# mLSTM scan and MLP on one core: two groups more with divided words, one copy in place of two halves, and a new written order

## The chip, the cores and the metric

The kernel runs on one core of a Trainium2 chip. The metric is device time in microseconds (us). Before the change the median of three runs is 465.06 us (464.52 to 466.18). The engines are TensorE (PE, with its weight loads apart as PEld), VectorE (DVE), ScalarE (ACT), GpSimd (POOL) and SyncE (SP), whose queue issues most DMA transfers.

## What is computed

The first half is a recurrent attention with gates, for 4 batches, 8 heads, 768 steps and a head size of 40:

```python
m_new = maximum(f[t] + m, i[t])
f_stab, i_stab = exp(f[t] + m - m_new), exp(i[t] - m_new)
C = f_stab * C + i_stab * outer(v[t], k[t])
n = f_stab * n + i_stab * k[t]
y[t] = sigmoid(o[t]) * (C @ q[t]) / maximum(abs(n . q[t]), 1)
```

The second half takes the 3072 rows of y, 320 wide, through two layers:

```python
h = x @ w_in            # 320 x 2048
g = h * erf(softplus(h))
out = g @ w_out         # 2048 x 320
```

w_in and w_out come as 64-bit floats, whose two 32-bit words the kernel turns into float32 itself.

## The kernel before

The scan is cut into 12 steps `k` of 64 time steps. In each step `attention` works on batch rows 0 and 1 and then on rows 2 and 3: scores, masks, products with the carried state, and the state's update. Its result is divided, gated, turned on PE and kept as `xh` and `xl`, a rounded part and the rest. `mlp(g)` takes a quarter `q` of the 2048 hidden columns for one step, so there are four groups to a step; for steps 0 and 1 they alternate (`k, q = g % 2, g // 2`). A group multiplies up (L764, "up"), copies to `hb` (ACT L775), takes softplus (ACT L784), erf (ACT L788) and the product (DVE L792), and multiplies down into a sum over four groups ("dn"), for two halves `b` of 128 rows each.

A down multiplication has two forms, and `PLAIN` chooses. Groups below it use float32 words whole, four matmuls a half (L828). The others divide their words first: `gh` is `n0` rounded (ACT L802, or DVE L804 from group 32 on) and `gl` is the rest (DVE L808). Then eight matmuls "hi" of a half take `gh` with both parts of w_out (L832, L833) and four "lo" take `gl` with w_out's rounded part (L830). w_out's blocks are divided by `split_out`, all 16 of them. The sums of a step lie in the PSUM tiles `pob0` and `pob1`, but that of step 1 lies in a buffer of the pool `pa`, of which there are two; the scores, products and turned results use the same two.

The order of the work is written out. `Plan` collects some 1,590 operations with the engine and the dependences of each; `ORDER` (L94 on) lists their numbers, and `plan.run` emits them in that order. Each engine works through its own instructions in that order, and waits where a needed one is not done. A negative number stands for filler matmuls (`stay`, L910). ACT's functions come from tables; where the next operation needs another one, a table load (L913) is emitted.

The startup: `gate_block` makes the gates' sums of two steps (DVE L311 to L317), which go through DRAM (`gd`, L378) to be spread as masks `dm` and factors `eT`. `weights_in` and `weights_tail` turn w_in's words (DVE L640, ACT L646, DVE L651) and split them into `wh` (ACT) and `wl` (DVE L665, L703). `vg` (DVE L495) is the gated v, L578 masks scores, `qe` (DVE L478) is q with its factors, L516 the state's matmuls, L405 makes `xl`'s part of a turned result. `kvo` (L439) is one transfer of k, v and the output gate.

At the end of a step each half of the sum is copied to SBUF on ACT (L859) and stored in two pieces on SP's queue (L865). For the second half of the last step there is another way: ACT copies 160 columns (L844) and issues a store on its own queue (L845), DVE copies the others (L849), and SP stores them (L853).

Of the kernel before, what the change touches and what calls it, by code (L numbers as in the profile page):

```python
# [17 lines left out]
L = 64  # L18
# [15 lines left out]
class Plan:  # L34
# [135 lines left out]
def tile_mlstm_moe(  # L170
# [561 lines left out]
    def mlp(g):  # L732
# [77 lines left out]
        for b in range(2):  # L810
# [24 lines left out]
            if q == 3:  # L835
                def rows(x, b):
                    return x.rearrange("(b s) e -> b s e", s=S)[2 * b:2 * b + 2, k * L:(k + 1) * L]

                if k == NC - 1 and b == 1:
                    half = DM // 2  # L840

# [133 lines left out]
```

## Time and profile before

| what | before |
|---|---|
| median of three runs | 465.06 us |
| lowest, highest | 464.52, 466.18 us |
| the profiled execution's own time | 466.24 us |
| its span, first to last instruction | 464.5 us |
| mean granted TensorE clock | 0.983 |
| busy in the span: PE, ACT, DVE, POOL | 450.7, 338.0, 334.0, 38.3 us |
| matmuls | 6000 |

How to read it: the busy time of an engine is the time in which it had an instruction at work; a PE that is busy may still run at the lower clock. The chain is followed back from the last instruction, at each step to what released it. The granted clock is a share of the full one, 2.4 GHz. Line numbers are those of the kernel before; in the new kernel they are one higher, and 20 lower behind the removed lines.

### The profile page before, as it was taken

Reading aid. Unit: us, or ns where it says so; the run is one execution under the profiler, and the core shown is the slowest. Engines: PE = TensorE matmul, PEld = TensorE weight load, DVE = VectorE, ACT = ScalarE, POOL = GpSimd, SP = SyncE. Lnnn points to the kernel's source line nnn. Section 1 sums busy time; section 2 is a strip of 40 time slices with the busy share of each in tenths; the row PEclk is TensorE's granted clock in tenths of the full one; section 3 lists DMA queues with packets and bytes.
Section 4 is the critical chain, followed back from the end, with each engine's and each line's share of the span. In section 5 each row is a group of like instructions: output and inputs, shape, how many; then the busy total and the mean of one; then the engine's idle time right before and its main releaser. Section 6 shows DMA issues by size and latency. Waiting matters only on the chain.

```text
span 464.5 us, 13909 instructions
## 1 busy us (share of the span) xinstructions
PE 450.7 (97%) x6000; PEld 405.0 (87%) x6000; DVE 334.0 (72%) x658; ACT 338.0 (73%) x530; POOL 38.3 (8%) x64
## 2 busy tenths in 40 slices
PE   6989998999999999999999999999999999999995
PEld 4669996788899998999999898899899889999994
DVE  5889788854878667887766867786678885567651
ACT  4568997966998875786877695987866776776550
POOL 4002010012120020003102000104001000000000
PEclk9879998999999999999999999999999999999999
DMA  7899595671841112147160464015522100000111
GB/s 212 326 276 344 167 251 193 178 256 28 250 129 49 48 39 78 22 135 191 30 181 0 107 214 126 3 48 155 135 71 65 31 1 17 14 2 8 22 30 28
DMA packets 46930, 51.80 MB, mean 112 GB/s; under 512 B 27028, under 2 KB 31764, under 8 KB 46868
## 3 DMA queue, kind: packets, MB, share of 16 engines
q1 hardware_dynamic: 46738, 50.83, 37.5%
q8 instruction: 47, 0.77, 0.7%
q14 instruction: 15, 0.12, 0.1%
q10 hardware_dynamic: 130, 0.08, 0.1%
HBM read 46.77 MB, written 4.13 MB: 110 GB/s over the span
## 4 chain that ended last, share of the span: by engine, by line
PE 94%; DVE 2%; DMA 2%; ACT 1%; issue 1%; DVEq 0%
PE h L764 40%; PE pob L832 11%; PE pob L830 11%; PE pob L833 10%; PE pa L536 3%; PE pa L828 3%; PE pa L516 3%; PE pa L507 2%; PE pa L521 2%; PE pob L828 2%; DMA kvo<-in_kvo_dram 1%; PE pa L388 1%; PE pa L444 1%; PE pob L282 1%; PE pa L529 1%
## 5 line engine op out<-in xcount | busy, mean ns | idle before, releaser
L764 PE MATMUL h<-xh,wh 128*128 128x256 f32 (+1 forms) x768 | 202.2, 347 | 0.1
L764 PEld LDWEIGHTS h<-xh,wh 128*128 128x128 f32 x768 | 127.6, 193 | 13.5 <-DVE hb L780 0.5
L775 ACT ACTIVATE hb<-h 128x256 f32<-128x256 f32 (+1 forms) x160 | 66.5, 421 | 69.9 <-PE h L764 69.6
L764 PE MATMUL h<-xh,wl 128*128 128x256 f32 x384 | 109.2, 284 | 0.0
L832 PE MATMUL pob<-woh,gh 128*128 128x320 f32 x328 | 98.8, 313 | 0.0
L833 PE MATMUL pob<-wo,gh 128*128 128x320 f32 x328 | 97.5, 309 | 0.0
L780 DVE TENSOR_TENSOR hb<-h,hb 128x256 f32<-128x256 f32 x128 | 52.3, 420 | 48.3 <-ACT hb L775 47.2
L913 ACT ACT_TABLE_LOAD x62 | 79.5, 1283 | 1.8 <-PEq L963 0.8
L764 PEld LDWEIGHTS h<-xh,wl 128*128 128x128 f32 x384 | 73.8, 192 | 2.3 <-DVE wl L665 0.2
L792 DVE TENSOR_TENSOR n<-n,hb 128x1024 f32<-128x1024 f32 x48 | 58.3, 1219 | 14.6 <-ACT n L788 14.4
L833 PEld LDWEIGHTS pob<-wo,gh 128*128 128x128 f32 x328 | 61.7, 188 | 1.5
L832 PEld LDWEIGHTS pob<-woh,gh 128*128 128x128 f32 x328 | 61.8, 188 | 0.7
L830 PE MATMUL pob<-woh,gl 128*128 128x320 f32 x328 | 60.7, 311 | 0.0
L485 POOL TENSOR_SCALAR_AFFINE_SELECT dm<-dm 128x512 f32<-128x512 f32 (+1 forms) x40 | 32.6, 821 | 311.0 <-ACT dm L465 279.1
L830 PEld LDWEIGHTS pob<-woh,gl 128*128 128x128 f32 x328 | 52.3, 188 | 1.6
L808 DVE TENSOR_TENSOR gl<-n,gh 128x1024 fp32r<-128x1024 f32 x42 | 51.6, 1230 | 1.1 <-ACT gh L802 0.7
L784 ACT ACTIVATE n<-hb 128x1024 f32<-128x1024 f32 x48 | 50.0, 1058 | 1.9 <-DVE hb L780 1.5
L788 ACT ACTIVATE n<-n 128x1024 f32<-128x1024 f32 x48 | 49.9, 1055 | 0.3
L802 ACT ACTIVATE gh<-n 128x1024 fp32r<-128x1024 f32 x26 | 27.1, 1057 | 0.7 <-DVE n L792 0.7
L405 DVE TENSOR_TENSOR xh<-pa,xh 128x384 fp32r<-128x384 f32 x24 | 13.3, 554 | 19.1 <-ACT xh L401 19.1
L536 PEld LDWEIGHTS pa<-kvo,dm 64*32 64x32 f32 x1408 | 15.6, 109 | 4.3 <-issue 3.7
L578 DVE TENSOR_TENSOR dm<-pa,dm 128x512 f32<-128x512 f32 x22 | 15.0, 683 | 5.8 <-PE pa L507 5.2
(103 smaller groups left out, 486.3 us busy)
## 6 DMA issues: line engine op xcount, KB each, us to landing
qk<-in_qk_dram SPq DMA_DIRECT2D x24, 512.0 KB, 3.7
kvo<-in_kvo_dram SPq DMA_DIRECT2D x24, 484.0 KB, 5.2
eT<-gd SPq DMA_DIRECT2D x44, 128.0 KB, 3.7
raw<-in_w_out_dram SPq DMA_DIRECT2D x16, 320.0 KB, 7.4
dm<-gd SPq DMA_DIRECT2D x40, 128.0 KB, 3.2
raw<-in_w_in_dram SPq DMA_DIRECT2D x8, 512.0 KB, 8.1
out_dram<-o SPq DMA_DIRECT2D x47, 80.0 KB, 2.1
raw<-in_w_in_dram SPq DMA_DIRECT2D x4, 256.0 KB, 7.4
```

The source lines that it names most:

```text
L485: nc.gpsimd.affine_select(out=x, in_=x, pattern=[[0, H], [1, L]], compare_op=ALU.is_ge, fill=0.0, base=base, channel_multiplier=-1)
L764: nc.tensor.matmul(h[:, n * T:n * T + n_], w, m, start=(s == 0), stop=(s == len(ops) - 1))
L775: nc.scalar.activation(part(), G(f'h{i}')[:, T:2 * T] if wide else G(f'h{i}'), AF.Copy)
L780: nc.vector.tensor_tensor(part(), G(f'h{i}')[:, 0:T], part(), op=ALU.add)
L784: nc.scalar.activation(new('n0', [128, 1024], ('n0', g)), G('hb'), AF.Softplus)
L788: nc.scalar.activation(G('n0'), G('n0'), AF.Erf)
L792: nc.vector.tensor_tensor(G('n0'), G('n0'), G('hb'), op=ALU.mult)
L808: nc.vector.tensor_tensor(new('gl', [128, 1024], ('gl', g), F32R), G('n0'), G('gh').bitcast(F32), op=ALU.subtract)
L830: nc.tensor.matmul(acc(b), G('gl')[:, ts], woh[:, j], start=False, stop=(j == NFF - 1))
L832: nc.tensor.matmul(acc(b), G('gh')[:, ts], woh[:, j], start=(j == 0), stop=False)
L833: nc.tensor.matmul(acc(b), G('gh')[:, ts], t['wol', j], start=False, stop=False)
L913: plan.run(ORDER, lambda k: nc.scalar.preload_act_table_set(KIND[k]), stay)
```

## The change

`PLAIN` goes from 6 to 4: groups 4 (step 0) and 5 (step 1), third quarter, now divide their words. With `PLAIN` the places move where `split_out` is written: blocks 8 to 15 ahead of group 4, and 0 to 7 behind group 7. The other way of the last half's copy is taken out. `ORDER` is written anew throughout; it has four filler matmuls in place of three, and it makes 62 table loads in place of 61.

```diff
 ORDER = [
-    2, 10, 4, 41, 0, 5, 9, 12, 1, 13, 6, 3, 7, 14, 15, 8, 16, 11, 17, 33, 34, 32, 36, 31, 25, 343, 344, 20, 27, 28, 18, 35, 19,
...
+    0, 5, 2, 1, 3, 41, 7, 9, 11, 12, 13, 14, 15, 4, 20, 25, 31, 6, 16, 10, 8, 17, 351, 352, 33, 34, 26, 27, 28, 30, 24, 38, 37,
...
 ]
-PLAIN, JOIN, GH_ACT, FLAT = 6, 3, 32, 1
+PLAIN, JOIN, GH_ACT, FLAT = 4, 3, 32, 1
...
-                def rows(x, b):
-                    return x.rearrange("(b s) e -> b s e", s=S)[2 * b:2 * b + 2, k * L:(k + 1) * L]
-
-                if k == NC - 1 and b == 1:
-                    half = DM // 2
-
-                    @op('ACT', 0.2, r=[(po(b), b)], w=[(('o', k, b), 0)], tile_=('o', ('o', k, b)))
-                    def _(b=b):
-                        nc.scalar.activation(new('o', [128, DM], ('o', k, b))[:, 0:half], acc(b)[:, 0:half], AF.Copy)
-                        nc.scalar.dma_start(rows(out, b)[:, :, 0:half], t['o', k, b][:, 0:half])
-
-                    @op('DVE', 0.2, r=[(po(b), b)], w=[(('o', k, b), 1)], tile_=())
-                    def _(b=b):
-                        nc.vector.tensor_copy(t['o', k, b][:, half:DM], acc(b)[:, half:DM])
-
-                    @dma(320, mm=8, r=[(('o', k, b), 1)])
-                    def _(b=b):
-                        nc.sync.dma_start(rows(out, b)[:, :, half:DM], t['o', k, b][:, half:DM])
-
-                    continue
-
```

The order moves at two places that matter below. The first is DVE in the startup. Before, this is what stands there up to the low part of w_in's columns 0 to 511, rows 0 to 127 (`raw_408`); `raw_303` holds rows 128 to 255 of these columns, `raw_251` the tail rows 256 to 319, `raw_487` and `raw_495` the next columns:

```order
L578 TENSOR_TENSOR dm_321<-pa_333,dm_321 128x2x4x64
L623 SCALAR_TENSOR_TENSOR kvo_157<-kvo_157 128x320
L495 TENSOR_TENSOR vg_387<-kvo_385,dm_325 128x328
L578 TENSOR_TENSOR dm_325<-pa_353,dm_325 128x2x4x64
L478 TENSOR_TENSOR qe_393<-qk_327,eT_390 104x512
L405 TENSOR_TENSOR xh_280<-pa_395,xh_280 128x3x128
L665 TENSOR_TENSOR wl_74<-raw_303,wh_73 128x512
L640 TENSOR_SCALAR raw_408<-raw_408 128x512
L703 TENSOR_TENSOR wh_73<-raw_251,wh_73 64x512
L651 SCALAR_TENSOR_TENSOR raw_408<-raw_408 128x512
L405 TENSOR_TENSOR xh_280<-pa_412,xh_280 128x3x128
```

Now, with `raw_277` and `raw_322` for the two parts of the same columns, `raw_261` for the tail and `raw_378` and `raw_381` for the next columns:

```order
L496 TENSOR_TENSOR vg_332<-kvo_328,dm_330 128x328
L406 TENSOR_TENSOR xh_297<-pa_334,xh_297 128x3x128
L666 TENSOR_TENSOR wl_74<-raw_277,wh_73 128x512
L406 TENSOR_TENSOR xh_297<-pa_345,xh_297 128x3x128
L641 TENSOR_SCALAR raw_322<-raw_322 128x512
L479 TENSOR_TENSOR qe_356<-qk_343,eT_353 104x512
L579 TENSOR_TENSOR dm_330<-pa_358,dm_330 128x2x4x64
L704 TENSOR_TENSOR wh_73<-raw_261,wh_73 64x512
L641 TENSOR_SCALAR raw_378<-raw_378 128x512
L652 SCALAR_TENSOR_TENSOR raw_322<-raw_322 128x512
L652 SCALAR_TENSOR_TENSOR raw_378<-raw_378 128x512
L641 TENSOR_SCALAR raw_381<-raw_381 128x512
```

The two `xh` operations stand ahead of the first `wl`, one gated v and one masked score in place of two stand ahead of them, and the second `wl`, from `raw_322`, follows right behind these rows.

The second place is SP's queue around the load of step 2's kvo for batch rows 0 and 1. Before, it is `kvo_1038`; `gd4` are the stores of the gates of steps 4 and 5, `raw` the loads of w_out, `gt` a load of gates:

```order
L378 DMA gd4_851<-x_775 8x4x64
L292 DMA gt_889<-in_gates_dram 128x2x128
L473 DMA eT_891<-gd2_402 64x8x64 x2
L435 DMA qk_894<-in_qk_dram 128x2x512
L473 DMA eT_949<-gd2_402 64x8x64 x2
L711 DMA raw_1021<-in_w_out_dram 128x640
L711 DMA raw_1024<-in_w_out_dram 128x640
L456 DMA dm_1034<-gd2_402 64x512 x2
L378 DMA gd4_851<-x_775 8x4x64
L439 DMA kvo_1038<-in_kvo_dram 128x968
```

Now it is `kvo_1139`:

```order
L712 DMA raw_964<-in_w_out_dram 128x640
L436 DMA qk_1089<-in_qk_dram 128x2x512
L379 DMA gd4_1108<-x_750 8x4x64
L474 DMA eT_1110<-gd2_723 64x8x64 x2
L293 DMA gt_1132<-in_gates_dram 128x2x128
L379 DMA gd4_1108<-x_750 8x4x64
L712 DMA raw_1137<-in_w_out_dram 128x640
L440 DMA kvo_1139<-in_kvo_dram 128x968
```

Two stores of gates stand ahead of the load in either order; one of the two mask and factor loads went elsewhere, and a w_out load stands directly ahead.

## Rows read from the trace of the kernel before

**Rows 1.** The page: busy time by engine, and shares of the last chain.
```profile
PE 450.7 (97%) x6000; PEld 405.0 (87%) x6000; DVE 334.0 (72%) x658; ACT 338.0 (73%) x530; POOL 38.3 (8%) x64
...
PE 94%; DVE 2%; DMA 2%; ACT 1%; issue 1%; DVEq 0%
```

**Rows 2.** Stretches: length, busy of PE, PEld, DVE, ACT, POOL, clock, DMA share, GB/s.
```profile
50.00:60.00 10.00, 10.00 (x110) 9.80 (x110) 7.88 (x18) 9.92 (x20) 0.00 (x0) 1.00 0.46 111
...
70.00:80.00 10.00, 7.87 (x154) 6.65 (x154) 8.32 (x19) 7.49 (x14) 0.00 (x0) 0.84 0.57 194
250.00:260.00 10.00, 10.00 (x146) 8.88 (x145) 7.46 (x13) 7.01 (x15) 2.91 (x4) 1.00 0.14 34
...
29.03:35.86 6.83, 6.83 (x145) 6.43 (x142) 6.56 (x13) 4.90 (x11) 0.00 (x0) 0.50 0.96 220
76.80:80.20 3.40, 3.40 (x17) 3.40 (x18) 2.99 (x7) 3.38 (x9) 0.00 (x0) 0.50 0.71 231
```

**Rows 3.** The chain of waits: start, length, what; an up, and down pieces.
```profile
82.46 1.91 PE h L764 x16
84.37 2.15 PE pa L828 x8
...
457.10 0.15 PE pob L832
...
458.28 0.60 PE pob L830 x4
```

**Rows 4.** The page's groups: operation, count, busy, mean ns, idle before it.
```profile
L913 ACT ACT_TABLE_LOAD x62 | 79.5, 1283 | 1.8 <-PEq L963 0.8
...
L792 DVE TENSOR_TENSOR n<-n,hb 128x1024 f32<-128x1024 f32 x48 | 58.3, 1219 | 14.6 <-ACT n L788 14.4
...
L808 DVE TENSOR_TENSOR gl<-n,gh 128x1024 fp32r<-128x1024 f32 x42 | 51.6, 1230 | 1.1 <-ACT gh L802 0.7
L784 ACT ACTIVATE n<-hb 128x1024 f32<-128x1024 f32 x48 | 50.0, 1058 | 1.9 <-DVE hb L780 1.5
L788 ACT ACTIVATE n<-n 128x1024 f32<-128x1024 f32 x48 | 49.9, 1055 | 0.3
L802 ACT ACTIVATE gh<-n 128x1024 fp32r<-128x1024 f32 x26 | 27.1, 1057 | 0.7 <-DVE n L792 0.7
```

**Rows 5.** DVE's timeline, 15 to 34 us: start, length, operation, idle before it.
```profile
15.20 0.28 DVE L311 TENSOR_TENSOR x<-gt,m 128x128 f32<-128x128 f32 x1
...
24.43 0.69 DVE L651 SCALAR_TENSOR_TENSOR raw<-raw 128x512 int32<-128x512 int32 x1 [1.27 <-ACT raw L646]
...
27.04 0.69 DVE L578 TENSOR_TENSOR dm<-pa,dm 128x512 f32<-128x512 f32 x1 [0.51 <-PE pa L392]
...
29.77 0.68 DVE L703 TENSOR_TENSOR wh<-raw,wh 64x512 fp32r<-64x512 f32 x1
...
32.70 0.68 DVE L665 TENSOR_TENSOR wl<-raw,wh 128x512 fp32r<-128x512 f32 x1
```

**Rows 6.** The chain of waits in the startup: filler matmuls, first up matmuls.
```profile
11.70 1.05 PE pob L910 x2
...
32.91 5.43 PE h L764 x32
```

**Rows 7.** The chain of waits from 63 to 75 us.
```profile
63.77 6.64 DMA kvo<-in_kvo_dram
...
70.50 0.51 DVE vg L495
...
74.82 0.68 PE pa L516 x32
```

**Rows 8.** The timeline of the last 12 us: start, length, operation, idle before it.
```profile
452.31 0.69 DVE L804 CAST gh<-n 128x1024 fp32r<-128x1024 f32 x1
...
454.60 0.31 PE L832 MATMUL pob<-woh,gh 128*128 128x320 f32 x1
...
458.90 0.44 ACT L859 ACTIVATE o<-pob 128x320 f32<-128x320 f32 x1 [2.04 <-PE pob L830]
```

139 rows, old and new, of the table ORDER are left out of this document.

## Prediction

> **What bounds the kernel now.** I read the page first. TensorE (PE) is busy 97% of the span of 464.5 us and holds 94% of the chain that ended last [rows 1]. So the time is PE's own work, plus the places where PE stands or runs at half clock. The table by stretches tells where these are [rows 2]. From 250 to 260 us PE is busy 10.00 of 10 at full clock, while VectorE (DVE) has 7.46 and ScalarE (ACT) 7.01: in such a stage nothing is gained but by taking work off PE. From 70 to 80 PE is busy 7.87 and the mean granted clock is 0.84. From 29.03 to 35.86 and from 76.80 to 80.20 the clock is 0.50, the lower level of 1.2 GHz, each time after idle time of PE. The chain then shows the work of the steady stage, the first up matmuls and the stall near 70 us [rows 3, 6, 7]; DVE's timeline shows what the first up matmuls wait for [rows 5].
>
> **The change, part by part.**
>
> *Two groups more are split.* A whole-word down projection of one half takes 2.15 us (its four matmuls are eight records) [rows 3]. A split one starts at 457.10 with its eight matmuls "hi", and its four "lo" start at 458.28 and take 0.60 [rows 3]: 1.18 + 0.58 = 1.76 us. Two groups of two halves each are four such pieces: 4 x (2.15 - 1.76) = **1.56 us** less of PE work, on the path, since PE is the path. Between neighbouring pieces nothing else is loaded or stored. All sixteen blocks of w_out are split in either kernel, so no work is added there, it only comes earlier for blocks 8 to 11.
>
> What it adds: two copies to gh on ACT, 1.06 each, and two subtractions to gl on DVE, 1.23 each [rows 4]; the new order also holds one table load more, 1.28 [rows 4]. That is 3.4 us on ACT and 2.5 on DVE. I cost them at nothing: what hides them is the room that both have in most stages (7.01 and 7.46 of 10). Where that cover is thin is 50 to 60 us, where ACT is busy 9.92 of 10 [rows 2]; if all of ACT's 3.4 fell there and PE had no work in hand, that is what it would cost. One filler matmul more (four in place of three), half of 1.05 [rows 6], stands where PE waits for DVE anyway; 0.53 if it did not.
>
> By the row, a whole-word matmul is worth 2.15 / 4 = 0.54 us and a one-pass one 0.147. The Trainium skill, FP8 and Floating Point Precision, section TensorE Precision Notes, counts four passes through the array for true FP32; three passes in place of four would save a quarter of 2.15, 2.15 us over the four pieces, and the forecast would be 0.6 us lower. The rows say 18%, and I go by them.
>
> *The startup.* The first up matmuls are in the chain at 32.91 [rows 6]. They need both halves of the turned x (xh) and the decoded w_in, both finished by DVE. Before, DVE starts the second block of gates at 15.20 and ends the low part (wl) of w_in's first 128 rows at 32.70 + 0.68 [rows 5]: 36 instructions in 18.2 us, in which it waits 1.27 for ACT and 0.51 for PE [rows 5]. In the new order the same two points are 32 instructions apart: four of a later use come behind (one combination of the w_in words 0.69, one tail row 0.68, one masked score 0.69, one gated v 0.51 [rows 5, 7]), 2.6 us in all. Two xh operations moved ahead of the decoding, so what PE's first up matmuls wait for is the second wl. The bounds: 2.6 if both waits of 1.8 us stay, 4.4 if both go. My walk through both engines' new order with the durations of this trace puts the first up matmul at 29.7, a gain of **3.2**, between them; PE's own first pieces start 0.3 later, as one small DVE operation moved ahead of them, and this is in it.
>
> I deduct 1.0 for the clock. Of the 32 matmuls that take 5.43 from 32.91 [rows 6], each 16 cost 1.91 at full clock [rows 3], so half clock cost them 1.6; whether the stretch comes again, and how much of it falls on heavy matmuls, the trace can't tell. Between 0 and 1.6 lost anew I take a little over half, since PE still stands for DVE in the new order. Startup: **-2.2**, bounds -1.0 (2.6 less 1.6) and -4.4.
>
> *The stall at 70 us.* The load of step 2's kvo for batch rows 0 and 1 is issued on SyncE's queue (SP) only at 63.77 and takes 6.64 to land; then come the gated v (0.51), a masked score, the state and qe before PE's state matmuls at 74.82 [rows 7]. PE loses 10 - 7.87 = 2.1 in that stretch, and the 3.40 us at half clock cost another 1.7 [rows 2]: 3.8 us. On SP this load stood behind two w_out loads, a mask load and two stores of the gates of steps 4 and 5, which DVE has to finish first. In the new order it still stands behind two such stores, a gate load and two w_out loads; its place in the queue is no better, but I count DVE 4.6 us ahead of PE there, where before the two were level (an estimate: the durations of this trace added up along each order). So the stall goes. What is late next are ACT's exponentials and masks for batch rows 2 and 3, with ACT near full from 50 to 60 [rows 2]; I give **1.0** back for them, between 0 and the 2.5 that would be two thirds of the old stall. Term: **-2.8**, bounds -3.8 and -1.3.
>
> *The steady part.* From 82 to 458 us PE shows no wait; the pieces are the same but for the four above, and the new order changes from one kind of matmul to the other about as often. Cost 0, bounds -0.5 and +0.5, a filler matmul either way.
>
> *The last copy.* The removed half copies and their stores belonged to the half that ended second to last. The very last piece was already a one-piece copy on ACT at 458.90, 0.44 long, with two SP stores behind it [rows 8]; this stays, only the halves are exchanged. The removed work ran beside PE. Nothing. PE's last group: DVE starts its gh copy at 452.31, done 0.69 later, and PE's first matmul with it starts at 454.60 [rows 8], so 1.6 us are spare; in the new order there is one piece of 0.58 less between the last up matmuls and that place, and 1.0 remains.
>
> **Sum.** -1.56 - 2.2 - 2.8 = -6.5 on the span: 464.5 to 458.0. The profiled run took 466.24 on the same account, so it would take 459.7; the median of the runs, 465.06, is 1.2 lower, and the forecast for the median is 465.06 - 6.5 = **458.6**. With all terms at their small ends (-1.56, -1.0, -1.3, +0.5) it is 461.7, with all at their large ends (-1.56, -4.4, -3.8, -0.5) 454.8.
>
> **Rivals.**
>
> B. *The clock takes the startup's gain.* The up matmuls begin earlier, but with shorter and more frequent waits between them, and the granted clock stays at 1.2 GHz longer. For it: 29.03 to 35.86 at 0.50 came straight after waits of PE [rows 2, 5]. Against it: from 35.86 on dense matmuls have the full clock in spite of the same neighbours. Price: the 2.2 of the startup gone, and up to 1.6 more for another 32 matmuls at half clock: 460.8 to 462.4. The Trainium skill, TensorE: Matmul & The Clock Gate, section A second HAM failure mode, says that frequent short idles between matmul groups make the clock oscillate; by that rule, B is what this order would get. The trace bears it out at two places only.
>
> C. *kvo is late again.* For it: the queue's order ahead of the load is no shorter than before. Against it: DVE's lead. If a store ahead of it waits for gates that DVE finishes no earlier than now, or SP for a free buffer, the load stays near 63.8 while PE comes earlier by the startup's gain. Then the old 3.8 stays, and the term of -2.8 goes: 461.4, and 462.4 if the small waits come on top.
>
> BC. *Both.* Only the PE work is saved: 465.06 - 1.6 = 463.5, and 465.1 with the half-clock matmuls of B. This is where the change would pass for no change.
>
> D. *Slower: the split groups hold up the scores.* Group 5 and group 7 add to step 1's sum, which sits in one of the two `pa` buffers in PSUM from its first down matmul to its last. Now group 5 needs gh and gl too. If PE comes to group 7's pieces before they are ready, it stands in order, the scores behind it too, for a chain of load, softplus, load, erf, product, gh and gl: 1.28 + 1.06 + 1.28 + 1.06 + 1.22 + 1.06 + 1.23 = 8.2 us [rows 4], and starts again at half clock, some 1.7 as at 76.80 [rows 2]. Lost: 9.9, against 6.5 gained: 468.5. It decides from 7.9 us of lost PE time on (6.5 + 1.4). For it: ACT at 9.92 of 10 just ahead. Against it: up matmuls of other groups stand between, and the same chain stalled PE nowhere after 82 us.
>
> **How the numbers follow.** Forecast 0.44, B 0.20, C 0.13, BC 0.12, D 0.11. The range takes the forecast, B and C (0.77) with their bounds, and the better half of BC: 454.8 to 464.4. A measurement of this kernel can tell 0.3% from no change, 1.4 us: below 463.7 is faster, above 466.4 slower. Faster: 0.44 + 0.20 + 0.13 and a sixth of BC, 0.79; same: the rest of BC, 0.10; slower: D, 0.11.
>
> **What would show it.** PE's busy time less by 1.6 plus what less time at half clock brings. The first up matmul in the chain near 29.7, and no idle of PE over 1 us between 65 and 80, with the step-2 kvo load issued before 60. A stretch at 0.50 that begins near 29 and lasts over 7 us would be B; a chain through the kvo load, C; idle time of PE ahead of down matmuls on gh or gl between 85 and 120 us, D. The prediction is wrong if PE's waits after 82 us, none now, come to more than 1.5 us: the steady part, which I cost at nothing, would then be the failed step.

## The result, and the profile after

| what | before | after |
|---|---|---|
| median | 464.93 us (4 runs) | 460.56 us (4 runs) |
| lowest, highest | 464.52, 466.18 | 459.35, 461.65 |
| profiled execution: own time, span | 466.24, 464.5 | 461.65, 459.9 |
| mean granted clock of that execution | 0.983 | 0.990 |

The ratio is 0.9889, with a 95% interval of 0.9862 to 0.9915: 4.4 us faster by the medians. The forecast was 458.6, or 6.5 us faster, with a range of 454.8 to 464.4.

The page of the changed kernel, to set against [rows 1], busy time by engine and shares of the last chain:

```profile
PE 448.7 (98%) x6018; PEld 403.9 (88%) x6018; DVE 339.0 (74%) x659; ACT 340.5 (74%) x533; POOL 41.4 (9%) x64
...
PE 83%; DVE 5%; ACT 5%; DMA 3%; SPq 1%; issue 1%; DVEq 0%; ACTq 0%
```

PE is still the bound. The chain leaves it more often: at 46.03 and at 85.93 us another engine was the last to release PE, and from there the chain runs back over DVE, ACT, SP's queue and a load, to 24.7 and to 68.1 us.

The stretches of [rows 2], and three more (length, busy of PE, PEld, DVE, ACT, POOL, clock, DMA share, GB/s):

```profile
17.80:24.20 6.40, 6.40 (x19) 3.84 (x18) 4.57 (x12) 2.85 (x6) 0.00 (x0) 0.50 1.09 303
50.00:60.00 10.00, 10.00 (x84) 9.82 (x83) 7.63 (x18) 9.52 (x19) 1.41 (x2) 1.00 1.05 230
70.00:80.00 10.00, 10.00 (x170) 7.86 (x169) 8.14 (x18) 8.63 (x13) 0.00 (x0) 1.00 0.87 220
80.00:90.00 10.00, 9.38 (x146) 7.72 (x145) 9.01 (x20) 9.89 (x14) 1.31 (x2) 1.00 0.86 201
250.00:260.00 10.00, 10.00 (x147) 8.94 (x146) 6.26 (x13) 6.59 (x12) 0.00 (x0) 1.00 0.02 4
29.03:35.86 6.83, 6.62 (x174) 5.71 (x167) 6.45 (x15) 4.51 (x8) 0.00 (x0) 1.00 1.00 285
76.80:80.20 3.40, 3.40 (x16) 2.45 (x15) 1.87 (x7) 2.06 (x5) 0.00 (x0) 1.00 1.04 273
```

From 70 to 80 us PE is now busy all the time and at full clock; 0.62 us of idle time come in the next ten. The two stretches that [rows 2] has at 0.50 are at 1.00. The clock is 0.50 from 17.80 to 24.20, before the heavy matmuls begin. The kernel before had a stretch at 0.50 there too, a shorter one, which [rows 2] leaves out:

```profile
18.80:22.20 3.40, 3.40 (x5) 1.35 (x5) 3.13 (x10) 2.01 (x4) 0.00 (x0) 0.50 0.74 263
```

The pieces of [rows 3] in the new chain of waits (start, length, what): a whole-word down, the first "hi" matmul of a half, and its four "lo".

```profile
101.97 2.15 PE pa L829 x8
...
115.50 0.15 PE pa L833
...
116.68 0.59 PE pa L831 x4
```

From the first "hi" to the first "lo" it is 1.18 us, and the piece behind starts at 117.26, 0.58 later: 1.76 in all, against 2.15. These are the durations that the sum went by.

The startup on DVE's timeline, to set against [rows 5]:

```profile
15.20 0.29 DVE L312 TENSOR_TENSOR x<-gt,m 128x128 f32<-128x128 f32 x1
...
25.26 0.56 DVE L406 TENSOR_TENSOR xh<-pa,xh 128x384 fp32r<-128x384 f32 x1 [1.94 <-ACT xh L402]
...
31.14 0.69 DVE L666 TENSOR_TENSOR wl<-raw,wh 128x512 fp32r<-128x512 f32 x1
```

and on PE's, where the first up matmul starts at 31.38, against 32.72 on the same view of before ([rows 6] has it at 32.91, where its share of the chain begins); the first line is the kernel before:

```profile
32.72 0.77 PE L764 MATMUL h<-xh,wh 128*128 128x256 f32 x2
...
30.82 1.12 PE L890 MATMUL pob<-ident 128*128 128x512 f32 x2
31.38 0.81 PE L765 MATMUL h<-xh,wh 128*128 128x256 f32 x2
```

The second block of gates starts at the same 15.20, and the second low part is done at 31.83 in place of 33.38. DVE still stood 1.94 us for a turned result. That it came late because PE ran at half clock is seen in another execution of the same kernel, `after_again` below, whose clock is 1.00 from 17 to 25 us: the products that take 3.08 us from 16.95 here (L530) take 1.98 there, and DVE goes on without a wait:

```profile
22.60 0.56 DVE L406 TENSOR_TENSOR xh<-pa,xh 128x384 fp32r<-128x384 f32 x1
```

The end, on the timeline, to set against [rows 8]:

```profile
454.03 3.46 SPq L845 DMA_DIRECT2D out_dram<-o  x4
455.91 0.44 ACT L839 ACTIVATE o<-pob 128x320 f32<-128x320 f32 x1 [1.91 <-PE pob L831]
```

From the start of the last copy to the end of the span it was 464.5 - 458.90 = 5.6 us; it is 459.9 - 455.91 = 4.0.

**Where the time went.** Each of PE's pieces (an up, a down, a step's scores and products) has a usual length, as in [rows 3]. They sum to 431.6 us before and 430.1 after. What PE takes from its first to its last matmul beyond that sum is worked out by stretch of the trace, with each piece's time up to the start of the next; fillers count as lost. Executions differ in the startup, so profiles of the experiments stand here too, where they left the stretch alone:

| stretch, us | old order | new order | difference of means |
|---|---|---|---|
| PE's pieces | 431.6 | 430.1 | -1.56 |
| lost, 0 to 50 | 13.5, 16.7, 14.5 | 12.9, 11.8, 13.2, 13.2 | -2.1 |
| lost, 50 to 92 | 4.5, 2.8 | 2.9, 2.7, 3.0 | -0.8 |
| lost, 92 to 125 | 1.2, 1.2 | 0.7, 0.8, 0.6 | -0.5 |
| lost, 125 to 300 | 3.2, 3.1, 3.2 | 4.3, 4.2, 4.4 | +1.1 |
| lost, 300 to the last matmul | 1.5, 1.5 | 1.4, 1.4, 1.4 | -0.1 |
| last matmul to the end | 5.6 | 4.0 | -1.6 |

The first number of each list is from the first pair of profiles. By these alone the startup gained only 0.6 and 50 to 92 us 1.6, and with PE's first matmul 0.2 later the sum is the 4.6 us between their spans. The means add up to 5.6, 1.2 more than the medians differ: the few profiled executions are no fair sample. The three of the old order took 0.7 to 1.5 us more than the medians of their kernels, the four of the new 0 to 1.1.

Four more profiles begin with the same startup (`plain6_after`, `hybrid500`, `hybrid700`, `vg_ahead_after`). Read in the same way they lost about 11.3, 12.0, 12.7 and 10.6 up to 50 us; with them the startup's gain is 2.7 on the mean, between single profiles from 10.6 to 13.2. By the first up matmul it is 2.1: it starts at 32.5 to 33.3 in the three profiles of the old order and at 29.8 to 32.1 in the eight of the new. `qe_first_before` is not in the row from 92 to 125 us: there PE stands 0.47 us ahead of 125.50, in a piece that begins before 125, without a wait that the profile shows. So the 0.5 of that row is less sure than its two equal numbers look.

### The profile page after: what moved, and what is told of

Same layout as the page of the kernel before. It is cut to its first block, busy times and chain, and to the rows that moved or that the text cites. A ratio compares the mean times of both kernels' runs of the same rounds, so it can differ in the third digit from the quotient of the medians.

```text
span 459.9 us, 13964 instructions
## 1 busy us (share of the span) xinstructions
PE 448.7 (98%) x6018; PEld 403.9 (88%) x6018; DVE 339.0 (74%) x659; ACT 340.5 (74%) x533; POOL 41.4 (9%) x64
## 4 chain that ended last, share of the span: by engine, by line
PE 83%; DVE 5%; ACT 5%; DMA 3%; SPq 1%; issue 1%; DVEq 0%; ACTq 0%
PE h L765 36%; PE pob L831 11%; PE pob L833 10%; PE pob L834 10%; PE pa L537 3%; PE pa L517 2%; PE pa L508 2%; PE pa L829 2%; ACT L893 2%; PE pa L522 2%; PE pa L389 1%; DMA raw<-in_w_out_dram 1%; DMA kvo<-in_kvo_dram 1%; PE pa L530 1%; ACT n L785 1%
## 5 line engine op out<-in xcount | busy, mean ns | idle before, releaser
L765 PEld LDWEIGHTS h<-xh,wh 128*128 128x128 f32 x768 | 125.4, 188 | 16.0 <-DVE xh L406 1.0
L765 PE MATMUL h<-xh,wl 128*128 128x256 f32 x384 | 107.8, 281 | 0.0
L833 PE MATMUL pob<-woh,gh 128*128 128x320 f32 x336 | 100.8, 312 | 0.0
L834 PE MATMUL pob<-wo,gh 128*128 128x320 f32 x336 | 99.9, 309 | 0.0
L486 POOL TENSOR_SCALAR_AFFINE_SELECT dm<-dm 128x512 f32<-128x512 f32 (+1 forms) x40 | 36.3, 914 | 305.3 <-ACT dm L466 289.1
L833 PEld LDWEIGHTS pob<-woh,gh 128*128 128x128 f32 x336 | 63.2, 188 | 0.6
L831 PE MATMUL pob<-woh,gl 128*128 128x320 f32 x336 | 62.3, 311 | 0.0
L809 DVE TENSOR_TENSOR gl<-n,gh 128x1024 fp32r<-128x1024 f32 x44 | 54.0, 1231 | 3.0 <-ACT gh L803 1.1
L803 ACT ACTIVATE gh<-n 128x1024 fp32r<-128x1024 f32 x28 | 29.4, 1053 | 0.9 <-DVE n L793 0.8
L406 DVE TENSOR_TENSOR xh<-pa,xh 128x384 fp32r<-128x384 f32 x24 | 13.1, 553 | 12.8 <-ACT xh L402 12.7
L479 DVE TENSOR_TENSOR qe<-qk,eT 104x512 f32<-104x512 f32 x22 | 16.0, 727 | 7.6 <-DMA eT<-gd 6.6
```

The lines of the kernel that those rows point to most:

```text
L486: nc.gpsimd.affine_select(out=x, in_=x, pattern=[[0, H], [1, L]], compare_op=ALU.is_ge, fill=0.0, base=base, channel_multiplier=-1)
L765: nc.tensor.matmul(h[:, n * T:n * T + n_], w, m, start=(s == 0), stop=(s == len(ops) - 1))
L809: nc.vector.tensor_tensor(new('gl', [128, 1024], ('gl', g), F32R), G('n0'), G('gh').bitcast(F32), op=ALU.subtract)
L831: nc.tensor.matmul(acc(b), G('gl')[:, ts], woh[:, j], start=False, stop=(j == NFF - 1))
L833: nc.tensor.matmul(acc(b), G('gh')[:, ts], woh[:, j], start=(j == 0), stop=False)
L834: nc.tensor.matmul(acc(b), G('gh')[:, ts], t['wol', j], start=False, stop=False)
```

## The experiments

Twelve kernels ran, in three groups on three chips. In the three groups the kernel before had medians of 465.06 (32 runs), 464.51 (11 runs) and 464.69 (35 runs), with single runs from 462.3 to 468.4, so differences below some 0.5 us are not told apart by medians. Where that is so, the stretch that an edit touches is read from its profile.

### The last copy

`tail_before` is the kernel before with the branch for the last half taken out, as in the change, and one number less:

```diff
...
-    1585, 1586, 1587, 1588, 1589, 1561, 1581, 1582, 1583, 1584,
+    1585, 1586, 1587, 1588, 1561, 1581, 1582, 1583, 1584,
```

> The kernel before, with nothing changed but the last step's second half: one ACT copy and two full-row stores on SP, in place of half copies and half-row stores on ACT's and SP's queues. Theory T (the half-row stores land late, at 463.2 in the trace of before, and hold back the two last stores, which land 4.0 us after issue in place of 2.0): 1.6 us less, all of it after the last matmul, and the two last stores land about 2.0 us after issue. Prediction's theory (the removed work ran beside PE and costs nothing): 0.0, span and tail as before.

`halves_after` is the changed kernel with that branch put back, for the half that now comes second to last:

```diff
+                if k == NC - 1 and b == 0:
+                    half = DM // 2
...
+                    continue
```

> The changed kernel with the half copies and half-row stores put back, for the half that now ends second to last. Theory T: 1.6 us more than the changed kernel, all of it after the last matmul, with half-row stores that land in fewer pieces and later than the full ones. The prediction's theory: no difference.

Measured: `halves_after` 462.46 (9 runs), 1.9 us over the changed kernel's 460.56, which ran on another chip. `tail_before` 464.68 against 465.06, ratio 0.9986 (0.9964 to 1.0008): 0.4 us less, where 1.6 was expected. The interval reaches from 1.7 less to 0.4 more, so the median alone shows neither theory. Its profiled startup lost 3.2 us more than that of before. The time behind the last matmul is clear of that. It is 5.61 us before and 5.57 in `halves_after`, 4.03 after and 4.02 in `tail_before`. What fills it is seen in the DMA view from 453 to 465 us, forty equal slices. The kernel before:

```profile
GB/s 0 0 0 0 0 0 0 0 0 0 0 0 0 0 0 0 0 17 45 45 26 26 13 13 45 53 149 250 207 45 45 49 45 21 0 0 0 0 0 0
...
q10 hardware_dynamic: 130, 0.08, 2.5%
```

and `tail_before`:

```profile
GB/s 0 0 0 0 0 0 0 0 0 0 0 0 0 0 0 0 0 0 0 0 0 0 107 162 73 192 13 0 0 0 132 141 115 158 0 0 0 0 0 0
```

(q10 is ACT's queue, with one half-row store, 80 KB.) While the half-row stores are alone on their way, the slices have 13 to 53 GB/s; when the full-row ones come they go up to 149 to 250, and in `tail_before`, with full-row stores alone, the full slices have 73 to 192. In the landings of the trace, the two half-row stores, issued at 456.88 (ACT's queue) and 457.24 (SP's), complete at 462.17 and 463.19, and each is reported in 3 parts; the full-row ones are reported in 16. The last two stores of before, issued at 459.36 and 459.93, land at 463.39 and 463.58, 4.0 and 3.7 us later; in the changed kernel the last two take 2.0 and 2.1. The parts tell more: of the last two stores of before, 14 of the 16 parts have landed by 461.82 and 462.06, 2.5 and 2.1 us after the issue, and only the last two come at 463.3 to 463.6, behind the half-row stores. Theory T holds in both directions: the half-row stores lay beside PE's work, as predicted, but their transfers had not ended when the last stores came.

### The divided words

`plain6_after` puts groups 4 and 5 back on whole words and keeps the rest of the new order (numbers shifted, since operations fall out):

```diff
-PLAIN, JOIN, GH_ACT, FLAT = 4, 3, 32, 1
+PLAIN, JOIN, GH_ACT, FLAT = 6, 3, 32, 1
```

> The changed kernel with groups 4 and 5 on whole words again, the order otherwise kept: their gh and gl operations left out, and the low parts of w_out's blocks 8 to 11 made after the last of these groups' down matmuls, since whole words keep their buffers longer. Theory W (the divided words save PE work, which is the path): 1.6 us more. Rival (DVE and ACT, freed of 4.6 us in the tight stretch, give it back): 0 to 0.5 us more.

Measured: 462.43 (12 runs), 1.9 over the changed kernel's first median. Its pieces sum to 431.6 us again, and the time lost up to the last matmul is 21.4, against 22.2 and 20.9 in two profiles of the changed kernel. So the 1.56 us are all there is, and nothing came back through DVE and ACT. The Trainium skill, FP8 and Floating Point Precision, section TensorE Precision Notes, counts four passes for true FP32, by which the saving, as an estimate, would have been 2.15; the rows of after, 2.15 against 1.18 + 0.58, agree with the smaller figure. The median alone, 1.9, would not tell 1.56 from 2.15.

### The stall at 70 us

`qe_first_before` moves the gated v (362) and the masked score (375) of step 2, rows 0 and 1, behind qe (359) in the kernel before:

```diff
...
-    354, 362, 373, 375, 378, 304,
+    354, 373, 378, 304,
...
-    180, 359, 490,
+    180, 359, 362, 375, 490,
...
```

> The kernel before, with two DVE operations of step 2, rows 0 and 1 (the gated v that waits for the kvo load, and the masked score) moved behind the state update, the divisions and qe that stood after them. Nothing is changed on SP. Theory Q (the stall at 70 us came of DVE's order: 3.3 us of work stood behind the wait for kvo): PE's wait of 2.1 and the stretch at half clock after it go, 3.0 to 3.8 us less. Prediction's theory (the load is late on SP): the load still lands at 70.4, and PE still waits; 0 to 1 us less.

`vg_ahead_after` does the reverse in the changed kernel: the divisions' start, the state update and qe (391, 394, 367) behind these two (370, 383). Number 722 moves by two places; the traces have ACT's instructions and SP's transfers in the same sequence in both kernels:

```diff
...
-    292, 293, 391, 394, 721, 498, 367, 179, 362, 246, 722, 150, 321, 370, 383, 301, 385,
+    292, 293, 721, 498, 179, 362, 246, 150, 321, 722, 370, 383, 391, 394, 367, 301, 385,
...
```

> The changed kernel with the gated v and the masked score of step 2, rows 0 and 1, put on DVE where the old order had them: ahead of the divisions, the state update and qe. Theory Q (DVE's order about the wait for kvo makes or removes the stall near 70 us): PE waits 1.0 to 2.5 us before that step's state matmuls, up to 2.5 us more in 68 to 92 us. Rival (the stall went with the load): no wait there, no difference.

Measured: `vg_ahead_after` 466.51 (12 runs), 6 us over the changed kernel and at 1.0025 of before (0.9998 to 1.0052): this one piece of DVE's order costs more than the whole change gained. PE loses 10.4 us from 68 to 92 us, where the changed kernel loses 2.3. Its stretches:

```profile
70.00:80.00 10.00, 8.15 (x157) 5.88 (x156) 7.79 (x16) 5.98 (x10) 0.00 (x0) 1.00 0.63 179
80.00:90.00 10.00, 6.01 (x26) 4.13 (x25) 5.84 (x13) 6.04 (x9) 1.31 (x2) 0.74 0.68 174
```

and DVE's timeline:

```profile
68.40 0.50 DVE L496 TENSOR_TENSOR vg<-kvo,dm 128x328 f32<-128x328 f32 x1 [2.19 <-DMA kvo<-in_kvo_dram]
...
70.61 0.50 DVE L633 TENSOR_TENSOR state<-state,pa 104x328 f32<-104x328 f32 x1
71.02 0.68 DVE L479 TENSOR_TENSOR qe<-qk,eT 104x512 f32<-104x512 f32 x1
...
83.79 0.78 DVE L641 TENSOR_SCALAR raw<-raw 128x320 int32<-128x320 int32 x1 [4.93 <-DMA raw<-in_w_out_dram]
```

DVE stands 2.19 us for kvo with the state update and qe behind it, and PE waits for qe (1.43 us idle at 71.85). That is the wait that was expected. That PE lost far more than the 2.5 us expected is due to what comes later, by a way that neither theory named: the chain of waits goes from the state update to SP, whose next load of factors (L474) had waited for it, through SP's queue to a w_out load issued at 76.53, and from its landing to DVE's shift at 83.79 and the turned result behind it. PE stands for that up to 85.70, and its clock is 0.50 from 84.85 to 91.68.

```profile
70.61 0.51 DVE state L633
...
71.25 0.63 SPq L474
...
76.53 7.24 DMA raw<-in_w_out_dram
...
83.79 0.78 DVE raw L641
```

The changed kernel's own chain takes the same way, in a milder form: from the state update (69.09) to SP's L474 (69.60), and to the w_out load that keeps DVE at 80.49. Its kvo load was issued 2.8 us later than in `vg_ahead_after` (65.81 against 63.03), and still this w_out load went out 2.0 us earlier and took 1.3 less:

```profile
74.57 5.90 DMA raw<-in_w_out_dram
```

DVE's timeline there has the state update and qe done when kvo lands, at 70.65:

```profile
69.09 0.50 DVE L633 TENSOR_TENSOR state<-state,pa 104x328 f32<-104x328 f32 x1
69.50 0.69 DVE L479 TENSOR_TENSOR qe<-qk,eT 104x512 f32<-104x512 f32 x1
...
70.95 0.49 DVE L496 TENSOR_TENSOR vg<-kvo,dm 128x328 f32<-128x328 f32 x1
```

though SP issues the load no earlier than before:

```profile
65.81 0.37 SPq L440 DMA_DIRECT2D kvo<-in_kvo_dram  x1
```

So Theory Q holds for the changed kernel: DVE's order makes the stall or removes it, and the load stayed late. But the same edit in the kernel before gave little: 464.55 (12 runs), ratio 0.9992 (0.9971 to 1.0013). Its loss from 68 to 82 us went from 3.7 to 0.3, as expected; yet that profile's PE had lost 1.8 us more between 35 and 68 us, and its state matmuls began at 74.52, where they had begun at 74.82. `tail_before`, with the old order there, had a smaller stall (1.1) after a still later start. In these profiles, one for each kernel, PE waited either before this place or at it. The time in [rows 7] was thus not a price that the removal pays out in full.

### The new wait at 84 us

After the change the up matmul at 84.79 waits for the turned results of step 2, rows 2 and 3, and ahead of these DVE stands 1.65 us for the w_out load just named. `late_shift` moves that shift (208) behind them:

```diff
...
-    387, 470, 208, 388, 389,
+    387, 470, 388, 389,
...
-    305, 398, 401, 462,
+    305, 398, 208, 401, 462,
...
```

> The changed kernel with one DVE operation, the shift of a w_out block that waits 1.65 us for its load at 80.5, moved behind the two turned results of step 2, rows 2 and 3. Theory L (the new stall ahead of the up matmul at 84.8 is this wait, passed on in order): the 1.2 us lost in that up matmul go, 0.8 to 1.2 less. Rival (the turned results are late for another reason, the gates' sums and the mask ahead of them): 0 to 0.4 less.

> The changed kernel as it is, timed beside the three that follow, since the startup differs from run to run. If the median of four runs (460.56) was a fair draw: 460 to 461, with a mean clock near 0.995; PE's time beyond its work up to 50 us near 12.5 us, from 125 to 300 us near 4.4.

Measured: 460.97 (6 runs) against 460.22 of the changed kernel (6 runs, mean clock 0.996, as expected) on the same chip. In the profile that up matmul lost 0.3 in place of 1.2, but from 50 to 92 us PE lost 3.0 in all, as without the edit (2.7 to 3.0). `after_again`, which has no edit, also lost 0.3 at that matmul, and 1.9 instead of 1.0 from 68 to 82. The wait is real, and removing it alone gains nothing: the rival's number came true. What takes the wait's place stands in both chains, a gap of PE within one down piece:

```profile
77.45 0.99 issue
...
75.81 0.76 issue
```

The first is `late_shift`, the second `after_again`; the first profile of the changed kernel has the same piece from 75.49 without a gap. "issue" means that the profile shows no wait there, so what makes the gap is not known.

### The startup

`no_third_filler` leaves out the filler that stood in the chain:

```diff
...
-    101, 103, 69, -1, 68, 70,
+    101, 103, 69, 68, 70,
...
```

> The changed kernel without the third filler matmul, which stands in the chain of its profile with 1.71 us at half clock, at 21.88. Theory S (a filler in a place where the next turn is already late is pure cost): 0.5 to 1.7 us less, all of it before 50 us. Theory H (the filler keeps the clock up for what follows): the mean granted clock falls below that of the changed kernel, 0.995, and the time is the same or up to 1.6 more.

`three` adds to this the late shift and the second block's decoding (102, 104, 105, 106) in DVE's idle time:

```diff
...
-    103, 69, -1, 68, 70, 74, 54, 57, 58, 99, 100, 67, 53, 55, 56, 102,
+    103, 69, 68, 70, 74, 54, 57, 102, 104, 58, 99, 100, 67, 53, 55, 105, 56,
...
-    76, 78,
+    76, 78, 106,
...
```

> Three edits of the changed kernel together: the third filler out, that shift moved, and the decoding of the second w_in block (shift, combination, rounding, rest) moved into DVE's idle time of 1.94 us at 23.3, ahead of the two turned results. Theory (DVE bounds the start of the up matmuls): first up matmul 1 us earlier or more, 1.5 to 3 us less in all. Rival (PE's pieces before it, or the clock, bound the start): no more than the late shift alone.

Measured: 459.95 and 461.08 (6 runs each) against 460.22, with single runs from 458.3 to 463.0: neither is told apart from the changed kernel. For the filler both theories stay open; the mean clocks over the runs, 0.994 without and 0.996 with it, differ by less than runs do. (The two kernels `hybrid500` and `hybrid500_nofill` further down differ in this filler alone, 12 runs each: 463.44 at a mean clock of 0.993 with it, 464.21 at 0.989 without. That leans to Theory H, but single runs lie from 461.3 to 466.9.) In `three` DVE did what was meant, and the second low part (at 25.87) was done five us earlier, but the first up matmul started at 31.04:

```profile
24.80 2.07 PE L445 MATMUL pa<-xd,lt 128*128 128x512 f32 x2 [0.16 <-DVE xh L406]
26.81 1.09 PE L517 MATMUL pa<-state,qe 40*64 40x41 f32 x32
...
30.11 1.49 PE L890 MATMUL pob<-ident 128*128 128x512 f32 x2
31.04 0.80 PE L765 MATMUL h<-xh,wh 128*128 128x256 f32 x2
```

That is the rival: with DVE out of the way, PE's own pieces ahead of it, at the clock they had, bound the start. The two records at 24.80 take 2.07 us, where four took 2.13 in the kernel before, at 8.19 and full clock: from 24.80 to 30.10 the clock is 0.50 in this profile.

### The steady part

`hybrid500` takes the new order up to 127.5 us and from there the old one for what is left; `hybrid700` changes over at 188 us; `hybrid500_nofill` is the first without the third filler. At the change-over of the first:

```diff
...
     347, 524, 405, 406,
-    286, 287, 314, 532, 315, 520, 522, 525,
+    741, 603, 602, 595, 604, 732, 731, 1245,
...
```

> The changed kernel's order up to its first 500 entries (127.5 us), and from there the order of the kernel before for all that is left. PE's time beyond its work from 125 to 300 us was 3.1 to 3.2 in three profiles of the old order and 4.2 to 4.4 in six of the new. Theory O (the new order itself costs 1.1 us there): 3.1 to 3.4 in that stretch, and 1 us less in all. Rival (the two groups' extra work on DVE and ACT or the earlier finish of the startup costs it): 4.2 to 4.4, no gain.

> As the first of these, with the old order only from entry 700 on (188 us). Theory O: the loss lies between 125 and 188 as well as behind it, so that from 125 to 200 it stays 2.2 to 2.4 and from 200 to 300 falls from 2.1 to 1.5; 0.5 us less in all.

> The same, and the third filler matmul left out. If both edits help: 0.3 to 1.5 us less than the one above; if the filler kept the clock: the same or more, at a lower mean clock.

Measured: 463.44, 466.36 and 464.21 (11 or 12 runs each): all three slower than the changed kernel's 460.2 to 460.6 on other chips; the kernel before had 464.69 beside them. From 200 to 300 us they lose 1.7, 1.5 and 1.7, where the new order loses 2.0 to 2.1 in every profile and the old 1.5. So the order itself costs about 0.5 there, as Theory O says. From 125 to 200 us they lose 5.7, 7.7 and 3.4, most likely because what each engine had in hand at the change-over didn't fit what followed: the stretch from 185 to 200 us of `hybrid700` has PE busy 11.27 of 15.00. For 125 to 200 us the test is void. One wait there is plain in the new order's profiles, after some scores near 138 us, where an up matmul stands for a buffer that ACT empties. PE's timeline in `after_again`:

```profile
138.62 0.51 PE L765 MATMUL h<-xh,wh 128*128 128x256 f32 x2 [0.49 <-ACT hb L776]
```

The profiles of the old order show no loss over 0.16 us at any piece from 125 to 300 us.

## Why the prediction was right, and where not

The direction and the range stood, and two of the sum's three terms, PE's work and the startup. The time was 2 us above the forecast: the third term, the stall, was much too large, and two terms put at nothing were not nothing.

- **PE's work, -1.56**: right. The pieces are 1.56 us less, and undoing it alone gave 1.9 by the medians. Its cover held: `plain6_after`, without two copies on ACT (2.1 of the 3.4 us) and the 2.5 on DVE, lost about as much of PE's time.
- **The startup, -2.2**: right in the mean, -2.1 to -2.7, with single profiles far apart. The first up matmul came at 31.38 in the profiled execution and at 29.91 in `after_again`, against 29.7 forecast. The bounds had DVE's waits of 1.8 stay or go. In the first profile they grew to 2.7 (0.73 and 1.94, both for pieces that PE made at half clock), and DVE's way to the second low part was 1.6 shorter; in `after_again` they went, and it was 4.4 shorter (15.37 to 29.17), the large bound. But there PE had a gap of 1.40 us of its own ahead of 29.14 ("issue" again), so that the start close to the forecast is in part luck. The working had DVE as the bound; `three` shows that PE's pieces and their clock bound it as much.
- **The clock, rival B**: its sign, a stretch at 0.50 that begins near 29 and lasts over 7 us, didn't come in the changed kernel. In the first profile half clock falls on 17.80 to 24.20 and can cost the light pieces there no more than half of these 6.4 us, while the first up matmuls run at full clock; in `after_again`, at 1.00 from 17 to 25 us, PE lost 1.1 less up to 50 us. The prediction counted two places at half clock in the trace of before; there were three. Over all runs the mean clock rose from 0.987 (before) to 0.995 and more, so the startup was not taken by it. The Trainium skill, TensorE: Matmul & The Clock Gate, section A second HAM failure mode, has frequent short idles swing the clock. No run here decides on that: in the startup the clock falls in some executions of one kernel and in others not, and after 92 us it falls in no profile but at the seams of the hybrids and in the last microseconds.
- **The stall at 70 us, -2.8**: the step that failed most. "DVE 4.6 us ahead of PE" was to let the load be issued early, "before 60". It was issued at 65.81, later than before, as rival C had it, and C's price didn't come, since DVE's order had moved the other work ahead of the wait. The stall did go, as forecast (no idle of PE from 65 to 80 us); but the mean gain from 50 to 92 us was 0.8, most likely because a wait at one place was partly the lateness that PE otherwise meets at another. The sum read the stall, less 1.0, as a price.
- **The steady part, 0**, for 82 to 458 us: from 125 to 300 us it was +1.1, outside its bounds of 0.5 either way; with -0.5 from 92 to 125 and -0.1 behind 300 it comes to +0.5, and the new wait at 84.79, which the table counts with the stall, stands in this stretch too. The prediction's own sign of being wrong, waits of PE over 1.5 us after 82, didn't come: PE is idle 0.95 us from 82 to 455, against 0.06 before. Of the +1.1, half is the one wait for ACT near 138 us, 0.4 to 0.6 in four profiles; 0.2 to 0.4 is that 35 to 37 pieces, in place of 33 or 34, lose some 0.1 where they begin or end. What makes them do so wasn't found.
- **The last copy, 0**: measured -1.6. The working asked whether the removed instructions lay beside PE, and not how long their transfers take. Their transfers were still on their way when the last stores came.
- **Rival D**: no sign of it in the changed kernel. From 92 to 125 us, where groups 5 and 7 add to step 1's sum, PE lost less, 0.7 in place of 1.2.

By the table the errors are 2.0 and 0.5 upward and 1.6 downward, so that 1.6 of 2.5 cancelled, which is luck. Without the 1.6 that the working put at nothing, the time would have been 462.2 by the medians, 3.6 over the forecast. The table leaves 1.2 of the difference between its sum and the medians open. Two slips in the prediction move no sum: its "sixth" of BC below 463.7 is an eighth, and the better half of BC ends at 464.3.

## What to carry to other kernels

Look behind an engine's wait for a transfer: what stands there, and which queue waits for that in turn. Here three operations in one order or the other about one late load were worth some 6 us, mostly by way of SP's queue. A stall in one profile is no price: compare what PE lost up to a later common point, in several executions. And follow the last stores to their landing, not to their issue.

## What the runs showed of the hardware

Two stores of 64 x 160 columns for two batches each moved at 13 to 53 GB/s together and took 5.2 to 6.0 us to land (`before`, `halves_after`, `qe_first_before`), each reported in 3 parts; stores of 64 full rows of 320 columns took 2.0 to 2.1 each, reported in 16 parts. While the slow ones were on their way, a full-row store took 3.6 to 4.0, and what came late were 2 of its 16 parts. The second queue is not what makes the few parts, since the half-row store on SP's queue had 3 as well; whether the half rows or the two batches in one access cause it was not tried apart.

One kernel has its stretches at half clock at different places in different executions: at 17.6 to 24.4 us in the first profile of the changed kernel, at none between 10 us and PE's last matmul in `after_again`, at 18.2 to 21.6 and 31.8 to 35.2 in `halves_after`, whose startup is the same.
